# Router on one NeuronCore: attention answers stored in token order, with a 12-byte list entry per token and choice

## The chip, the cores and the metric

The kernel runs on one core of a Trainium2 chip. The metric is the device time of one execution in microseconds; the time shown for a kernel is the median of its runs. The core has five engines that each run their own instructions in order: TensorE (PE, with weight loads listed as PEld), VectorE (DVE), ScalarE (ACT), GpSimd (POOL) and SyncE (SP, which here only issues transfers). Transfers that need a list of row numbers (gathers and scatters) are issued by POOL, the plain ones by SP. All of them are moved by the same 16 DMA engines.

## The reference, cut to what matters

There are two parts. The first is a delta-rule attention over 768 steps for 4 batches of 8 heads of width 48; its answers, as 3072 tokens of 384 numbers, are the input of the second. The second is a mixture of 8 experts: each token is sent to the two experts with the largest noisy logits.

```python
# attention, for each batch and head
for t in range(S):
    y[:, :, t] = einsum('bhd,bhde->bhe', q[:, :, t], state)
    v_old = einsum('bhde,bhd->bhe', state, kt)
    state = state + bt * einsum('bhd,bhe->bhde', kt, vt - v_old)
# x: 3072 tokens of 384 numbers, D = 384, E = 8, F = 1024
logits = x @ w_gate
noisy_logits = logits + log1p(exp(x @ w_noise)) * noise
top2 = the two largest of noisy_logits;  top2_w = softmax over these two
for e in range(E):
    out[tokens of e] += top2_w * (relu(x[tokens of e] @ w1[e]) @ w2[e])
```

All numbers are 32-bit floats.

## The kernel before

**The attention stage** cuts the 768 steps into 12 chunks of 64. A unit is one chunk of two batches, 128 tokens, and there are 24 units; a step is four units, and there are 6 steps (0 to 5). Each step needs an inversion of small triangular matrices, which is done on DVE column by column (`invert`, with `column` at L705 to L717), and then a recurrence from unit to unit (`recur`, L838). `answer` (L943) makes the 128 token rows of a unit: ACT copies them into a tile of the ring `ys` (L482), and PE turns them and multiplies them by the router's weights.

**The router** (`route`, L1022) works for two steps at once, then two, then one and one (`ROUTES`). It chooses two experts for each token, and counts how many earlier tokens chose the same expert, which gives each token a slot in each of its two experts' lists.

**The lists.** `rows_x` is a DRAM tensor of 8 x 3072 rows of 388 numbers: the token's row of 384, its number, its two gates and a code for its first expert. SP first clears the beginning of each expert's list, 512 rows and then 320 more, with rows of zeros whose token number is N, which means none (`clear`, L378; placed behind columns of the first two inversions at L1359 to L1366). POOL then writes every token's row to its two slots (`spread`, L385), 48 scatters of 128 rows of 1552 bytes.

**The order of the attention stage** is made when the program is built. Every piece of work is a job with an engine, a cost and what it reads and writes (`Jobs.add`, L111). `Jobs.order` (L141) plays the jobs through with these costs and puts them in a fixed order on each engine: of the jobs that can start within 0.02 us of the earliest, it takes the one with the smallest key. A job with `late` has a key behind all jobs without, so it is taken only where nothing else can start on its engine. PSUM is handed out as two single banks and three pairs of banks.

**The early tiles.** Expert 0's list is worked on in tiles of 128 rows. Five of them are done with late jobs while the last tokens are still routed (`early`, L1227): `EARLY` (L26) says after which step which tiles are begun; after step 3 tiles 0 to 3 in two batches, after step 4 tile 4. `cut` (L1188) leaves empty slots so that those tiles are full at that point. A batch loads its rows with SP (`load_rows`, L1238), DVE reads number and gate from them (`of_rows`, L1254), PE turns them and multiplies by w1 (`inner_of`) and w2 (`back`), DVE multiplies by the gate (L1320), and POOL scatters the result into `out` (`put_early`, L1212).

**The experts.** `rest` (L1644) does the last 192 rows of expert 0, and then the loop over experts 1 to 7 follows; each has 832 rows in six tiles of 128 and one of 64. The products are done in the manner of Strassen and Winograd, with sums of blocks of the weights (`add_up`, on POOL for the experts from 2 on) and of the rows. SP loads the next expert's rows in two plain transfers (`load_rows`, L1537), `places` (L1550) reads numbers and gates from them, `turn_rows` (L1560) turns them on PE for the next expert, POOL gathers the sums so far from `out` (`gather`, L416) and scatters the new ones (`scatter`, L425). PE, ACT, DVE and POOL run in the written order here, and in the attention stage PE, ACT, DVE and SP do; POOL's jobs there are linked one behind the other.

Of the kernel before, what the change touches and what calls it, by code (L numbers as in the profile page):

```python
# [25 lines left out]
EARLY = {3: [(0, 2), (2, 4)], 4: [(4, 5)]}  # L26
EARLY_TILES = 5
ROWS = TILES * 128 + MORE
ROW = 384 + 4
# [65 lines left out]
class Jobs:  # L95
# [123 lines left out]

    PATIENCE = 0.02  # L220
    SOON = 8.0

    def run(self, link):

        last = None
        for job in self.order():
            made = job.emit()
            if job.engine == self.POOL:
                made = [x if isinstance(x, mybir.Instruction) else x.ins for x in made]
                if last:  # L230
                    link(last, made[0])
                last = made[-1]
# [3 lines left out]
def kernel(  # L236
# [87 lines left out]

    rows_x = tc.dram_tile([E * N, ROW], FP32, name="rows_x")
    empty = const.tile([128, ROW], FP32, name="empty")
    nc.vector.memset(empty, 0.0)
    nc.vector.memset(empty[:, DM : DM + 1], float(N))

    number = const.tile([128, NCH, NU], FP32, name="number")  # L330
    for i in range(2):
# [3 lines left out]
        )  # L335

# [39 lines left out]
    written, cleared, added, early_out = [], {"clear": [], "clear_more": []}, [], []  # L376

    def clear(e, lo, hi, p):  # L378

        return nc.sync.dma_start(  # L380
            out=rows_x[e * N + lo : e * N + hi].rearrange("(t p) d -> p t d", p=p),
            in_=empty[0:p, None, :].to_broadcast([p, (hi - lo) // p, ROW]),
        ).ins

    def spread(rows, slot, cleared, of):  # L385
        d = nc.gpsimd.indirect_dma_start(  # L386
            out=rows_x,
            out_offset=bass.IndirectOffsetOnAxis(ap=slot, axis=0),
            in_=rows,
            in_offset=None,  # L390
        ).ins
        tc.declare_no_dep(d, group="spread", reason="no two tokens have the same row")
        tc.add_to_no_dep_group("spread", d)
        for i in cleared:
            tc.add_manual_dep(d, i.name, SYNC, reason="rows cleared before they are written")
# [3 lines left out]

    def gates_of(xr, e, gate):  # L400

        nc.vector.scalar_tensor_tensor(
            out=gate, in0=xr[:, :, DM + 3], scalar=float(e - E), in1=xr[:, :, DM + 2],
            op0=ALU.is_equal, op1=ALU.mult,
        )
        nc.vector.tensor_tensor(out=gate, in0=gate, in1=xr[:, :, DM + 1], op=ALU.add)
# [26 lines left out]
    def deltanet(ictx):  # L433
# [47 lines left out]
        NY = 3  # L481
        ys = ring([128, US, ROW], "y", NY)  # L482
# [460 lines left out]
        def answer(n, bank_y):  # L943
# [4 lines left out]
            y_n = ys(s)[:, i, 0:DM]  # L948
            y_key, xT_key = ("y", s % NY, i), ("xT", n % 2)
# [36 lines left out]
            )  # L986
# [240 lines left out]
        def early(s, lo, hi):  # L1227
# [10 lines left out]
            def load_rows(at):  # L1238
# [3 lines left out]
                for of, w in written:  # L1242
                    if of <= s:
                        tc.add_manual_dep(d, w.name, SYNC, reason="rows of the tokens so far")
# [641 lines left out]
```

## Time and profile before

| | |
|---|---|
| median of 14 runs | 827.26 us (823.19 to 838.1) |
| the profiled execution's own time | 828.71 us |
| its span, first to last instruction | 827.0 us |
| mean granted TensorE clock | 0.885 |
| busy: PE, DVE, POOL, ACT | 740.8, 571.7, 360.4, 332.3 us |
| moved | 93.82 MB |
| attention and routing, until about | 317 us |
| early tiles of expert 0 on PE alone, until | 373 us |
| the last rows of expert 0, until | 394 us |
| experts 1 to 7 | 60.7 us each, until about 818 us |

Times inside the execution are counted from the first instruction. "L1532" is line 1532 of the kernel. A line of the timeline gives start, duration, engine, line, what is written from what, how many, and in brackets how long the engine was idle before and what ended that. A line of the stages gives for a stretch of time each engine's busy time with the number of its instructions, the granted clock of TensorE, the busy share of the 16 DMA engines, and GB/s.

### The profile page before, as it was taken

How to read it: one execution, taken by the hardware profiler on the slowest of the kernel's cores; microseconds unless marked ns; L12 is line 12 of the kernel's file. 1: busy time of each engine (PE TensorE's matmuls, PEld its weight loads, DVE VectorE, ACT ScalarE, POOL GpSimd, SP SyncE). 2: the span in 40 equal slices, each digit the busy share in tenths (PEclk: the TensorE clock that was granted, in tenths of full speed). 3: DMA queues.
4: the chain of work that ended last, by engine and by line, in shares of the span. 5: the costliest groups of instructions: out<-in, count | busy, mean ns of one | idle time of the engine just before them, and what ended most of it. 6: DMA issues, size and time to landing. Idle time of an engine off the chain costs nothing.

```text
span 827.0 us, 22812 instructions
## 1 busy us (share of the span) xinstructions
PE 740.8 (90%) x9510; PEld 586.7 (71%) x9510; DVE 571.7 (69%) x1295; ACT 332.3 (40%) x789; POOL 360.4 (44%) x372
## 2 busy tenths in 40 slices
PE   3565788986988889999999999999999999999995
PEld 2355687876877778767578588588588597597593
DVE  5899698899899754007695686675675776776751
ACT  3557185765765543112430530531530531521500
POOL 1102010106320634302773873873883774784411
PEclk8655567677689869999999999999999999999998
DMA  2469866455632413632723523424324323201201
GB/s 46 77 115 337 180 122 164 120 133 134 214 67 42 128 61 118 241 106 86 262 78 102 155 77 109 147 77 129 125 78 152 99 77 117 76 20 42 59 30 34
DMA packets 119856, 93.82 MB, mean 113 GB/s; under 512 B 85414, under 2 KB 110023, under 8 KB 119744
## 3 DMA queue, kind: packets, MB, share of 16 engines
q1 hardware_dynamic: 108016, 64.54, 28.5%
q0 software_dynamic: 9552, 27.33, 9.8%
q8 instruction: 77, 1.26, 0.6%
q10 hardware_dynamic: 2176, 0.39, 0.3%
q14 instruction: 35, 0.29, 0.1%
HBM read 58.82 MB, written 34.81 MB: 113 GB/s over the span
## 4 chain that ended last, share of the span: by engine, by line
PE 46%; issue 5%; POOL 2%; ACT 0%; POOLq 0%; ACTq 0%
PE inner L1532 25%; PE outer L1532 15%; PE inner L1637 2%; PE inner L1564 2%; POOL out_dram L427 1%; PE inner L1675 1%; POOL sums L418 1%; PE outer L1685 1%; POOL t_w L1505 0%; PE outer L1690 0%; PE outer L1675 0%; ACT xe_r L1668 0%; PE outer L1664 0%; ACT hT L1679 0%; POOLq L427 0%
## 5 line engine op out<-in xcount | busy, mean ns | idle before, releaser
L1591 DVE TENSOR_TENSOR hT<-hT,inner 128x416 f32<-128x416 f32 x182 | 105.4, 586 | 61.2 <-PE inner L1532 53.8
L1597 ACT ACTIVATE hT<-inner 128x416 f32<-128x416 f32 x112 | 57.9, 517 | 171.4 <-PE inner L1532 170.7
L427 POOL DMA_INDIRECT out_dram<-sums,index x49 | 50.8, 1037 | 113.7 <-DVE sums L1432 105.3
L1432 DVE SCALAR_TENSOR_TENSOR sums<-outer,gate,sums 128x192 f32<-128x192 f32 x112 | 45.2, 414 | 50.2 <-PE outer L1532 50.2
L1532 PE MATMUL inner<-s_x,w1e 128*128 128x416 f32 x196 | 78.8, 513 | 0.0
L710 DVE TENSOR_TENSOR part<-t 128x30 f32<-128x30 f32 (+9 forms) x180 | 67.7, 376 | 4.5
L714 DVE TENSOR_TENSOR t<-t,part 128x30 f32<-128x30 f32 (+9 forms) x180 | 65.4, 363 | 6.2
L1586 ACT ACTIVATE hT<-hT 128x416 f32<-128x416 f32 x112 | 59.9, 547 | 12.1 <-DVE hT L1591 6.9
L386 POOL DMA_INDIRECT rows_x<-y,slot x48 | 49.3, 1026 | 33.1 <-issue 8.8
L679 POOL TENSOR_SCALAR_AFFINE_SELECT t<-t 128x1024 f32<-128x1024 f32 x6 | 7.6, 1267 | 119.8 <-DVE ss L650 119.8
L1532 PE MATMUL outer<-t_w,hT 128*128 128x192 f32 x336 | 59.7, 328 | 0.0
L1532 PEld LDWEIGHTS inner<-s_x,w1e 128*128 128x128 f32 x196 | 37.2, 190 | 31.4 <-issue 29.6
L1532 PE MATMUL inner<-xe,w1e 128*128 128x416 f32 x140 | 58.1, 513 | 0.0
L418 POOL DMA_INDIRECT sums<-out_dram,index x49 | 51.8, 1057 | 13.8 <-issue 12.4
L1532 PE MATMUL inner<-s_x,s_w 128*128 128x416 f32 x140 | 56.9, 512 | 0.0
L1532 PEld LDWEIGHTS outer<-t_w,hT 128*128 128x128 f32 x336 | 54.7, 190 | 0.4
L1569 ACT COPY xe<-inner 128x384 f32<-128x384 f32 (+1 forms) x49 | 20.1, 462 | 85.4 <-PE inner L1564 85.2
L1532 PE MATMUL outer<-w2e,hT 128*128 128x192 f32 x280 | 50.1, 326 | 0.0
L861 POOL TENSOR_TENSOR v<-v,norms 128x384 f32<-128x384 f32 x24 | 21.9, 930 | 60.9 <-DVE norms L693 30.4
L1532 PEld LDWEIGHTS outer<-w2e,hT 128*128 128x128 f32 x280 | 46.5, 190 | 2.2 <-issue 2.2
L1498 POOL TENSOR_TENSOR w1e<-w1e 128x256 f32<-128x256 f32 x54 | 46.2, 865 | 2.0
L1532 PEld LDWEIGHTS inner<-s_x,s_w 128*128 128x128 f32 x140 | 26.6, 190 | 22.3 <-issue 22.3
(209 smaller groups left out, 1639.9 us busy)
## 6 DMA issues: line engine op xcount, KB each, us to landing
w1e<-in_moe_w_dram SPq DMA_DIRECT2D x8, 1536.0 KB
w2e<-in_moe_w_dram SPq DMA_DIRECT2D x8, 1536.0 KB
xr<-rows_x SPq DMA_DIRECT2D x7, 1164.0 KB
rows_x<-empty SPq DMA_DIRECT2D x8, 776.0 KB
qp<-in_q_dram SPq DMA_DIRECT2D x48, 96.0 KB
v<-in_v_dram SPq DMA_DIRECT2D x48, 96.0 KB
out_dram<-empty SPq DMA_DIRECT2D x4, 1152.0 KB
kp<-in_k_dram SPq DMA_DIRECT2D x88, 48.0 KB
```

The source lines that it names most:

```text
L386: d = nc.gpsimd.indirect_dma_start(out=rows_x, out_offset=bass.IndirectOffsetOnAxis(ap=slot, axis=0), in_=rows, in_offset=None,).ins
L418: nc.gpsimd.indirect_dma_start(out=got, out_offset=None, in_=out, in_offset=bass.IndirectOffsetOnAxis(ap=index, axis=0), bounds_check=N - ...
L427: nc.gpsimd.indirect_dma_start(out=out, out_offset=bass.IndirectOffsetOnAxis(ap=index, axis=0), in_=got, in_offset=None, bounds_check=N - ...
L710: v_.tensor_tensor(out=part, in0=t[:, :, j + 1 :, j, None].to_broadcast(shape), in1=t[:, :, None, j, 0:j].to_broadcast(shape), op=ALU.mult,)
L714: v_.tensor_tensor(out=t[:, :, j + 1 :, 0:j], in0=t[:, :, j + 1 :, 0:j], in1=part, op=ALU.add)
L861: lambda: [nc.gpsimd.tensor_tensor(out=v_n, in0=v_n, in1=norms(s)[:, i * H : (i + 1) * H, None].to_broadcast([128, H, D]), op=ALU.mult,)],
L1432: nc.vector.scalar_tensor_tensor(out=got, in0=p, scalar=gate, in1=got, op0=ALU.mult, op1=ALU.add)
L1498: engine.tensor_tensor(out=block(to), in0=block(x), in1=block(y), op=ALU.add if sign == "+" else ALU.subtract,)
L1532: nc.tensor.matmul(p, lhsT, rhs, start=opens and i == 0, stop=i == len(products) - 1, skip_group_check=True,)
L1586: nc.scalar.activation(h, h, ACTF.Relu)
L1591: nc.vector.tensor_tensor(out=h, in0=h, in1=p, op=ALU.add if sign > 0 else ALU.subtract)
L1597: nc.scalar.mul(h, p, float(sign))
```

## The change

The token rows are no longer carried in the lists. Each unit's answers are stored once, by SP, in a tensor `rows_y` of 3072 rows in the order in which they are made. A list entry (`tokens_x`) is now 12 bytes: token number, gate, and place in `rows_y`. One transfer fills all lists with empty entries. The experts load the entries (`load_metas`), DVE converts numbers and places to integers for all experts at once (`numbers`), and POOL gathers the rows by place, a tile at a time (`take_rows`). The code for the first expert and the arithmetic on it go, since an entry belongs to one choice and holds its own gate. `EARLY` begins tiles 0 and 1 after step 1. The zeroing of `out` moves from steps 2 and 4 to steps 1 and 2. The ring `ys` has four tiles of one unit each instead of three of four units. Two more tiles are zeroed by DVE at the start of the experts, since entries that are empty gather nothing. POOL's jobs in the attention stage are in the written order as those of the other engines.

```diff
-EARLY = {3: [(0, 2), (2, 4)], 4: [(4, 5)]}
+EARLY = {1: [(0, 2)], 3: [(2, 4)], 4: [(4, 5)]}
-ROW = 384 + 4
+META = 3
...
-    def clear(e, lo, hi, p):
-        return nc.sync.dma_start(
-            out=rows_x[e * N + lo : e * N + hi].rearrange("(t p) d -> p t d", p=p),
-            in_=empty[0:p, None, :].to_broadcast([p, (hi - lo) // p, ROW]),
+    def blank(tile):
+        blanked.append(
+            nc.sync.dma_start(
+                out=tokens_x.rearrange("(p t) c -> p t c", p=128), in_=tile
+            ).ins
+        )
+    def store(n, y_n):
+        d = nc.sync.dma_start(out=rows_y[n * 128 : (n + 1) * 128], in_=y_n).ins
+        tc.declare_no_dep(d, group="taken", reason="rows of other tokens were read")
+        stored.append((n, d))
+    def take_rows(got, index, units):
+        d = nc.gpsimd.indirect_dma_start(
+            out=got, out_offset=None, in_=rows_y[0 : units * 128],
+            in_offset=bass.IndirectOffsetOnAxis(ap=index, axis=0),
+            bounds_check=units * 128 - 1, oob_is_err=False,
         ).ins
+        tc.add_to_no_dep_group("taken", d)
+        for n, i in stored:
+            if n < units:
+                tc.add_manual_dep(d, i.name, SYNC, reason="rows stored before they are read")
+        return d
...
-        NY = 3
-        ys = ring([128, US, ROW], "y", NY)
+        NY = 4
+        ys = ring([128, DM], "y", NY)
...
+            jobs.add(
+                SP, 0.7, lambda: store(n, y_n), reads=[y_key], writes=[("stored", n)],
+                lands=2.0, moves=0.7,
+            )
...
-                        lambda x=x, of=of, i=i, to=to: [spread(
-                            ys(of)[:, i], to[:, x : x + 1],
-                            [y for name in clears for y in cleared[name]], of,
-                        )],
+                        lambda x=x, of=of, y=y, to=to: [
+                            spread(metas(g)[:, x, y], to[:, x : x + 1], of)
+                        ],
-                        due=FIRST + (s + paced) * PACE + BEHIND + 5.0, apart=4.5 / steps * paced,
+                        due=FIRST + (s + paced) * PACE + BEHIND + jobs.AFTER,
+                        apart=jobs.APART * paced,
...
+            jobs.add(
+                SP, 0.7, load_meta, reads=of_steps, writes=[("early_meta", lo)], lands=2.0,
+                moves=0.3, late=lo,
+            )
+            jobs.add(
+                DVE, 0.4, numbers, reads=[("early_meta", lo)], writes=[("early_index", lo)],
+                late=lo,
+            )
...
                 jobs.add(
-                    SP, 0.7, lambda at=at: load_rows(at), reads=of_steps,
+                    POOL, 1.2,
+                    lambda x=x, at=at: [take_rows(x, early_place[:, at : at + 1], units)],
+                    reads=[("early_index", lo), *(("stored", i) for i in range(units))],
                     writes=[x_key], lands=2.0, moves=0.7, late=lo,
                 )
...
-        for e in range(E):
-            for name, at, span in (
-                ("clear", (0, e * 4 + 1), (0, EARLIEST, 128)),
-                ("clear_more", (1, e * 3 + 2), (EARLIEST, ROWS, MORE)),
-            ):
...
+        behind(0, 20, 0.7, 1.0, lambda: blank(blanks), ["blank"])
-                (2, 4)[i // 2], (27, 29, 4, 16)[i], 0.7, 4.0, lambda i=i: clear_out(i),
+                (1, 2)[i // 2], (7, 22, 7, 22)[i], 0.7, 4.0, lambda i=i: clear_out(i),
...
-        for got in sums:
-            nc.gpsimd.memset(got, 0.0)
+        for got in (xrs[0], xrs[1], *sums):
+            (nc.vector if got in xrs else nc.gpsimd).memset(got, 0.0)
...
+        def numbers(e, t):
+            nc.vector.tensor_copy(places[:, e, t], metas[:, e, t, 2])
+            nc.vector.tensor_copy(indices[:, e, t], metas[:, e, t, 0])
+        def load_rows(e, tiles=range(TILES + 1)):
+            for i in tiles:
+                take_rows(
+                    xrs[e % 2][0 : rows_in[i], i], places[0 : rows_in[i], e, i : i + 1], NT
+                )
...
+            for e in range(E):
+                load_metas(e)
+            numbers(slice(0, 1), slice(t0, TILES + 1))
+            load_rows(0, range(t0, TILES + 1))
+            numbers(slice(1, E), slice(0, TILES + 1))
             load_rows(1)
             add_up(nc.vector, SUMS_W, blocks[0])
...
             if follows:
-                load_rows(e + 1)
                 weights = load_weights((w_even_tiles, w_odd)[(e + 1) % 2], e + 1)
                 blocks = blocks_of(*weights)
...
             first(a1, iter(of_hidden[0]))
             if follows:
+                load_rows(e + 1)
                 add_up(nc.gpsimd, SUMS_W, blocks[0])
```

The lists for tokens beyond the 832th of an expert (a branch at the end of the program) are changed in the same way; the branch is entered only where an expert has more rows than that. In this input the fullest expert has 807 tokens.

## The prediction

> **What bounds the kernel now.** I read the stages first, then who waits in each, then the timeline around every place the change touches. The columns are busy time with the number of instructions per engine, granted clock, DMA share and GB/s:
>
> ```profile
> 60.00:100.00 40.00, 26.08 (x800) 23.25 (x804) 32.09 (x74) 18.92 (x48) 4.99 (x5) 0.50 0.95 263
> 200.00:250.00 50.00, 42.95 (x1346) 37.60 (x1338) 45.49 (x108) 35.24 (x93) 19.18 (x20) 0.76 0.50 142
> 340.00:374.00 34.00, 32.27 (x150) 24.21 (x149) 2.72 (x8) 6.25 (x18) 2.96 (x3) 1.00 0.49 170
> 455.00:516.00 61.00, 61.00 (x288) 45.95 (x287) 42.17 (x76) 19.29 (x39) 41.08 (x40) 1.00 0.36 114
> ```
>
> Three regimes. Until about 280 us DVE sets the pace (third busy number: 45 of 50). From 316 us PE does, first with the early tiles of expert 0 (32 of 34), then with the experts, where it never rests. The chain that ended last agrees: back to 374 us it is nearly all PE. So time is won only by freeing DVE before 280 or by taking work from PE after 316.
>
> In the first stretch the DMA engines are full (0.95), and this shows in waits of PE and then DVE:
>
> ```profile
> PE pair L852 <- issue: 4.6, 1, 4.6
> PE pair L956 <- issue: 2.3, 1, 2.3
> DVE st L931 <- PE pair L919: 6.4, 2, 6.1
> ```
>
> PE's work after 316, from the timeline; the first batch (tiles 0 and 1) is the first two lines, most of it:
>
> ```profile
> 317.80 7.94 PE L1284 MATMUL pair<-early_xe,w1e 128*128 128x256 f32 x36
> 329.28 10.48 PE L1308 MATMUL pair<-w2e,early_hT 128*128 128x384 f32 x32
> 340.66 10.63 PE L1284 MATMUL pair<-early_xe,w1e 128*128 128x256 f32 x48 [0.57 <-ACT early_xe L1273]
> 368.02 5.33 PE L1308 MATMUL pair<-w2e,early_hT 128*128 128x384 f32 x16
> 373.38 0.62 DVE L1320 TENSOR_SCALAR early_x<-pair,early_gate 128x384 f32<-128x384 f32 x1 [11.05 <-PE pair L1308]
> 374.36 0.15 DVE L1470 CAST most_i<-most 128x1 int32<-128x1 f32 x1
> 375.23 4.67 POOL L1480 MEMSET sums<- 128x2688 f32 x2
> 375.51 5.14 PE L1675 MATMUL inner<-xe_r,w1e 128*128 128x192 f32 x30 [0.50 <-ACT xe_r L1668]
> ```
>
> The reader is to see that expert 0's last rows start at 375.51, 2.16 us after PE's last early matmul (368.02 + 5.33 = 373.35, called T), as their rows were loaded long before.
>
> **Lists: clears go, stores come.** Out go 8 x (776 + 485) KB = 10.1 MB that SP issues from 60 to 107 us. In come 0.3 MB of empty entries, 24 stores of 192 KB from 81 us on, and the 4.6 MB that zero `out`, drawn forward from 133 to 217. I put about 5.5 MB in the old clears' stretch, so the queues are no longer full, and I expect DVE's 6.1 us wait at 94 to 100 to shrink to about 1: **-5 us** (ends: 0, as "issue" names no cause, and -9.2, the waits 2.3 + 2.3 + 4.6 of PE at 77 to 90). A store takes SP about 0.67 us (four v loads took 2.67) and waits for ACT's copy; behind it on SP stand q, k and v loads, and POOL's v products and then DVE wait for those. SP often waits on PE for their buffers anyway: **0**, ends 0 and +5 (the nearest row: POOL's v product waited 3.99 us for its v before 113.81). The zeroing of `out` is four issues of 0.66, moved ahead of loads of steps 2 and 3 on SP; only the early scatters wait for it, which come after 225: 0. The router loses one DVE subtraction of 0.17 per route and POOL four small copies: 0. The 48 scatters stay 48 at 0.97 us; only their pieces shrink.
>
> **Tiles 0 and 1 begin after step 1.** Their 7.94 + 2.84 + 10.48 = 21.3 us of PE leave the stretch after 316: **-21.3**. They go beside the recurrences at 225 to 316, where PE is idle about 7 of 50 us, at a clock of 0.76. Their weights are there (issued at 146.7 and 163.8), the 16 scatters of steps 0 and 1 ran from 192.7 to 215 with one at 233. With them go 8 ACT relus of 0.38, two DVE products of 0.62, two casts of 0.15, four POOL transfers of 1.0. What it costs there is not shown. Ends: -2 (steadier matmuls lift the clock: 1.00 in all of 316 to 374) and +21.3 (nothing hidden). Three in-order queues are crossed: on SP the entry load waits for the last of the 16 scatters to land, with v and q loads of step 4 behind it (before, such loads held SP 50.8 us in all with nothing behind them); on POOL the gathers and two scatters stand among v products; on DVE the casts among columns. I take **+3.5**, nearest the lower end: 21.3 us of jobs of about 1.3 us, each of which can hold back a recurrence step, with DVE's columns as cover while they last (to 277).
>
> **Tiles 2 and 3 take one hop more.** Now SP loads rows and PE turns them. Then: entries, two casts, a gather of 1.0 us, 3.1 us to land. The entries land as the rows did (313.1); casts 0.3, signal 0.3, gather and landing 3.1, the second 1.3 later, against a fourth row load that landed at 315.5: **+3** (ends 0, and +9 where seven scatters of 1.27 are put first on POOL). POOL's scatters of step 4, which wait here for the reads of the list (7.46 us idle until 316.31), still do. Tile 4 waited for the buffer of tile 0; it no longer does: 0.
>
> **Expert 0's last rows now wait for DVE and POOL after T.** `numbers` and `take_rows` stand behind the early jobs on in-order engines. DVE: product and counts to T+1.2, then two zeroings of 128x2688, by POOL's row of that shape 2.35 each, to T+5.9, casts to T+6.3. POOL: scatter, then its own two zeroings (375.23 + 4.67) to T+6.6; gathers issue at T+6.6 and T+7.9, land 3.1 later at T+11.0; transpose 0.5, copy 0.3, signals 0.4: matmuls start at T+12.2, not T+2.2: **+10** (ends +8, landing 2.5 and faster zeroing, and +14, landing 6.7, the slowest of that row). PE's clock falls in such a gap: after the last matmul (817) it is 0.54 on average in 821 to 827; and it climbs from 0.50 through 0.81 to 1.00 in 304 to 316, one 4-us slice: **+2**, ends 0 and +4. Expert 1's seven gathers follow to T+18.3 and land by T+21.4; PE wants them from T+12.2+8.1 on, tile by tile: 0. The eight entry loads are about 6500 pieces of 12 bytes. The 16 k loads of the first 10 us are 4096 pieces of 192 bytes at a DMA share of 0.46, at most 18 ns each on one engine: 7.3 us over 16 engines, between the last scatter's landing (341) and T: 0.
>
> **Experts 2 to 7: seven gathers more on POOL.**
>
> ```profile
> 412.20 0.95 POOL L418 DMA_INDIRECT sums<-out_dram,index  x1 [0.30 <-DVE s_h L1520]
> 413.18 1.41 POOL L1498 TENSOR_TENSOR w1e<-w1e 128x256 f32<-128x256 f32 x2
> 420.58 1.54 POOL L1498 TENSOR_TENSOR s_w<-w1e,s_w 128x256 f32<-128x256 f32 x2 [4.58 <-PE inner L1532]
> 437.95 1.00 POOL L427 DMA_INDIRECT out_dram<-sums,index  x1 [0.30 <-issue]
> 444.19 1.41 POOL L427 DMA_INDIRECT out_dram<-sums,index  x1 [5.24 <-DVE sums L1432]
> L418 POOL DMA_INDIRECT sums<-out_dram,index x49: 953/999/1417, 404.3 to 775.6; - x49
> ```
>
> 7 x 1.30 = 9.1 us stand before the weight sums. POOL waits 4.58 and 5.24 = 9.8 us there, so the third scatter still goes at about 444, and the sums end at 441 where the next expert starts at 455. The rows land by 426, PE turns the first at 430. Cost 0 (ends 0 and +2.2 an expert, if all gathers took 1.42: 7 x 0.42 less the 0.7 that is left).
> The Trainium skill speaks against this ("DMA: Bandwidth & Descriptors", SWDGE vs HWDGE vs iDMA): POOL writes the descriptors of its transfers to SBUF, and DVE can lock it out there in its two-port mode. Where the lock held each gather to the slowest shown, the sum would be 13 us worse; the row's median of 999 ns, beside a DVE busy 42 of 61, says it hardly does, and I go by the row.
> The same page (Rules for kernel authors) advises against many small transfers; it prices no 12-byte piece, so the 18 ns above stands.
>
> **Sum.** -5 - 21.3 + 3.5 + 3 + 10 + 2 = -7.8: the profiled 828.71 (span 827.0 and 1.7 around it) becomes 820.9. That execution lies 1.45 above the median, so I predict 819.5.
>
> **Rivals.**
> *Late jobs starve.* A late job runs only where its engine has nothing else. DVE is idle under 0.7 us in most 10-us slices from 225 to 280, so the casts of tiles 0 and 1 may come only after 277. The batch then fills PE's gaps at 280 to 316: in clock-weighted work PE does 22.4 of 36 us there, so 13.6 of 21.3 fit and 7.7 remain instead of 3.5: -3.6, or 824. For: DVE's fullness; against: the boundary of an inversion at 229 to 236, where DVE waits on ACT.
> *A pair of banks is held (the slower side).* The product that empties a tile's bank pair is a late DVE job too. If it waits for 277 while PE is done early, one or two of three pairs are lost to the recurrences of step 4, which need two at a time. Step 4's recurrence (236 to 282) would slip; at half of these 46 us the sum is -7.8 + 23 = +15: 842. It decides from 12 us of slip, where the sum passes +4. Against: the order is made with these costs.
> *The lists were hidden anyway and the hops are longer.* No gain from the clears, +9 and +14 at the upper ends: -21.3 + 3.5 + 9 + 14 + 2 = +7: 834.
> *More from the queues.* With -9.2, insertion at -2 and no hop: -21.3 - 9.2 - 2 + 10 + 2 = -20: 807.
>
> **How the numbers follow.** Forecast 0.40, own range 813 to 825; starved 0.22; pair held 0.18; hidden 0.12; more 0.08. Two runs of this kernel differ by about 0.5%, 4.1 us, and less can't be told from none. Faster: 0.9 of the forecast, 0.4 of starved, all of more: 0.53; slower: pair held, 0.9 of hidden, little of the rest: 0.30; same 0.17. The range leaves out the farthest of pair held and of more: 808 to 839.
>
> **What would show it.** No "issue" wait over 2 us at 77 to 95, and a DMA share under 0.8 there; L1284 before 280; matmuls of tile 2 within 4 us of the attention's last; PE idle about 10 us before L1675's successor with two DVE zeroings in it; experts at 60.7 us. Wrong, if attention ends more than 8 us from 317, or that gap is not 8 to 14.

## The result, and the profile after

The changed kernel takes 848.43 us (median; 843.29 to 858.02), the kernel before 829.36 (823.19 to 839.46): a ratio of 1.0238 (95% interval 1.0205 to 1.0270), 19 us slower. I had predicted 819.5 with a range of 808 to 839.

The profiled execution took 848.97 us, its span is 847.2, 20.2 more than before. Where they lie, from the timelines of both:

| place | before | after | adds |
|---|---|---|---|
| end of PE's last early matmul, T | 373.35 | 374.97 | +1.6 |
| from there to the first matmul of expert 0's last rows | 2.2 | 12.6 | +10.5 |
| those 30 matmuls | 5.14 | 7.78 | +2.6 |
| from the start of expert 1 to the last scatter | 423.2 | 423.6 | +0.4 |
| from the start of the last scatter to the end of the span | 9.6 | 14.7 | +5.1 |

The last column adds up to 20.2; between the third row and the fourth lie 13.6 us in both kernels. Of the five rows, two were in the prediction with about the right size (+10 and +2), the experts stood there with 0, T with -19.8, and the last row was not in it at all. The last scatter, first before, where the span is 827.0 us, then after:

```profile
817.44 0.98 POOL L427 DMA_INDIRECT out_dram<-sums,index  x1 [0.32 <-DVE sums L1432]
```
```profile
832.54 0.97 POOL L442 DMA_INDIRECT out_dram<-sums,indices  x1 [0.33 <-DVE sums L1439]
```

The view by stretches of the changed kernel (columns as before: busy time with instructions of PE, PEld, DVE, ACT, POOL, the granted clock, DMA share, GB/s):

```profile
60.00:100.00 40.00, 27.39 (x980) 24.41 (x983) 38.18 (x82) 22.42 (x58) 7.68 (x8) 0.67 0.57 146
...
200.00:250.00 50.00, 45.35 (x1204) 39.84 (x1206) 42.06 (x100) 31.30 (x86) 10.54 (x12) 0.64 0.22 47
340.00:375.00 35.00, 33.76 (x159) 25.18 (x157) 1.85 (x3) 6.63 (x19) 10.12 (x11) 1.00 0.38 109
375.00:388.00 13.00, 1.85 (x8) 1.28 (x8) 11.67 (x26) 0.79 (x2) 9.84 (x7) 0.67 0.20 47
470.00:531.00 61.00, 61.00 (x287) 45.69 (x286) 39.21 (x70) 19.29 (x39) 47.97 (x47) 1.00 0.35 112
```

The reader is to see this. With the clears gone the DMA share at 60 to 100 is 0.57 instead of 0.95, and DVE is busy for 38.2 us instead of 32.1. PE's stretch after the attention is as full as it was. And there is a new stretch, 375 to 388, in which PE does 1.85 us in 13 while DVE and POOL are busy. In an expert POOL works 48.0 of 61 us instead of 41.1, and PE rests as little as before.

Then the timeline of tiles 0 and 1 and of the time behind T (start, busy time, engine, line; in brackets the idle time before it and what ended it):

```profile
224.56 0.38 SPq L1257 DMA_DIRECT2D early_meta<-tokens_x  x1
279.40 0.12 DVE L1266 CAST early_place<-early_meta 128x2 int32<-128x2 f32 x1
288.06 1.05 POOL L396 DMA_INDIRECT early_x<-rows_y,early_place  x1 [0.31 <-issue]
290.74 1.05 POOL L396 DMA_INDIRECT early_x<-rows_y,early_place  x1 [0.30 <-issue]
320.25 9.31 PE L1310 MATMUL pair<-early_xe,w1e 128*128 128x256 f32 x42
330.43 10.57 PE L1334 MATMUL pair<-w2e,early_hT 128*128 128x384 f32 x32
342.28 10.63 PE L1310 MATMUL pair<-early_xe,w1e 128*128 128x256 f32 x48 [0.62 <-ACT early_xe L1299]
369.64 5.33 PE L1334 MATMUL pair<-w2e,early_hT 128*128 128x384 f32 x16
376.58 2.30 DVE L1491 MEMSET xr<- 128x2688 f32 x1 [0.51 <-DMA metas<-tokens_x]
376.86 4.65 POOL L1491 MEMSET sums<- 128x2688 f32 x2
379.39 2.30 DVE L1491 MEMSET xr<- 128x2688 f32 x1 [0.51 <-issue]
381.60 0.10 DVE L1561 CAST places<-metas 128x2 int32<-128x2 f32 x1
382.58 1.05 POOL L396 DMA_INDIRECT xr<-rows_y,places  x1 [1.08 <-issue]
385.82 1.39 PE L1672 MATMUL outer<-ident,xr 128*128 128x128 f32 x6 [10.74 <-DMA xr<-rows_y,places]
387.62 7.78 PE L1683 MATMUL inner<-xe_r,w1e 128*128 128x192 f32 x30 [0.41 <-ACT xe_r L1676]
```

The entries of tiles 0 and 1 are loaded at 224.6, 86 us earlier than their rows were before (310.6), as the change means it. Then they wait: DVE's casts come at 279.4, the gathers at 288 and 291, and PE's matmuls at 318 to 341, right where they were. The later lines are the stall: two zeroings on DVE, the casts, the gather, and PE idle for 10.74 us until the rows are there.

### The profile page after: what moved, and what is told of

Same layout as the page of the kernel before. It is cut to its first block, busy times and chain, and to the rows that moved or that the text cites. A ratio compares the mean times of both kernels' runs of the same rounds, so it can differ in the third digit from the quotient of the medians.

```text
span 847.2 us, 22977 instructions
## 1 busy us (share of the span) xinstructions
PE 748.6 (88%) x9512; PEld 591.2 (70%) x9512; DVE 556.6 (66%) x1240; ACT 332.1 (39%) x789; POOL 416.8 (49%) x432
## 3 DMA queue, kind: packets, MB, share of 16 engines
q0 software_dynamic: 11472, 27.31, 10.9%
## 4 chain that ended last, share of the span: by engine, by line
PE 63%; DVE 16%; issue 9%; ACT 3%; POOL 3%; DMA 2%; SPq 2%; POOLq 0%; DVEq 0%; ACTq 0%
PE inner L1543 24%; PE outer L1543 15%; DVE part L725 5%; DVE t L729 4%; PE pair L1310 3%; PE pair L1334 3%; PE pair L594 3%; PE inner L1647 2%; PE inner L1574 2%; DMA kp<-in_k_dram 1%; SPq L528 1%; PE single L986 1%; PE inner L1683 1%; DVE t L644 1%; PE pair L971 1%
## 5 line engine op out<-in xcount | busy, mean ns | idle before, releaser
L442 POOL DMA_INDIRECT out_dram<-sums,indices x51 | 54.7, 1072 | 99.0 <-DVE sums L1439 78.0
L1439 DVE SCALAR_TENSOR_TENSOR sums<-outer,metas,sums 128x192 f32<-128x192 f32 (+1 forms) x113 | 46.0, 416 | 63.8 <-PE outer L1543 62.9
L408 POOL DMA_INDIRECT tokens_x<-meta,slot x48 | 47.6, 991 | 76.7 <-DVE r_d L1058 40.2
L396 POOL DMA_INDIRECT xr<-rows_y,places x51 | 56.1, 1099 | 16.3 <-issue 15.4
L433 POOL DMA_INDIRECT sums<-out_dram,indices x49 | 51.2, 1046 | 13.9 <-issue 13.5
```

Of the source, the lines that this page charges most:

```text
L396: d = nc.gpsimd.indirect_dma_start(out=got, out_offset=None, in_=rows_y[0 : units * 128], in_offset=bass.IndirectOffsetOnAxis(ap=index, ax ...
L408: d = nc.gpsimd.indirect_dma_start(out=tokens_x, out_offset=bass.IndirectOffsetOnAxis(ap=slot, axis=0), in_=meta, in_offset=None, bounds_c ...
L433: nc.gpsimd.indirect_dma_start(out=got, out_offset=None, in_=out, in_offset=bass.IndirectOffsetOnAxis(ap=index, axis=0), bounds_check=N - ...
L442: nc.gpsimd.indirect_dma_start(out=out, out_offset=bass.IndirectOffsetOnAxis(ap=index, axis=0), in_=got, in_offset=None, bounds_check=N - ...
L1439: nc.vector.scalar_tensor_tensor(out=got, in0=p, scalar=gate, in1=got, op0=ALU.mult, op1=ALU.add)
```

## The experiments

Each one changes the kernel after unless it says otherwise. Two kernels with the same order in the attention can end it several us apart in their profiles (more on that below), so I read the effect in the stage first and the total second.

### The wait behind the last early matmul

Zero only what the first gathers need, and the rest behind them:

```diff
-        for got in (xrs[0], xrs[1], *sums):
-            (nc.vector if got in xrs else nc.gpsimd).memset(got, 0.0)
+        nc.vector.memset(xrs[0][:, EARLY_TILES:], 0.0)
...
             load_rows(0, range(t0, TILES + 1))
+            nc.vector.memset(xrs[1], 0.0)
             numbers(slice(1, E), slice(0, TILES + 1))
             load_rows(1)
+            for got in sums:
+                nc.gpsimd.memset(got, 0.0)
+            nc.vector.memset(xrs[0][:, 0:EARLY_TILES], 0.0)
```

> Theory (the stall after the early matmuls is real and sets the end): with only the two last tiles of the row buffer zeroed ahead of the gathers, and the other zeroings behind them, DVE reaches the casts about 2.0 us after the last early matmul instead of 6, the gathers go at 2.4 and 3.7, land by 6.8, and expert 0's last matmuls start 8 us after it instead of 12.6: 4 to 5 us less than the changed kernel, 843.5 to 844.5. Rival (expert 1's gathers, which then stand before POOL's zeroings of the sums, or something else behind the stall is late anyway): within 1.5 us of 848.4.

Measured: T at 379.30, the matmuls at 387.17, a gap of 7.9 us instead of 12.6, as the theory said. From T to the last scatter it takes 452.2 us instead of 457.6. The total did not show it: 848.99 us, ratio 1.0245 (1.0158 to 1.0333). In the profiled run the attention had ended 4.3 us later, 324.7 instead of 320.4, though the edit leaves the attention's order as it was. From its timeline:

```profile
380.51 0.70 DVE L1490 MEMSET xr<- 128x768 f32 x1
385.38 1.38 PE L1675 MATMUL outer<-ident,xr 128*128 128x128 f32 x6 [5.97 <-DMA xr<-rows_y,places]
```

So next the whole hop goes ahead of T: entries, casts and gathers of these rows become jobs behind the last list scatter, into two tiles of their own. The zeroings of `sums` and of the first row buffer go behind the gathers, and PE multiplies by w2 ahead of turning expert 1's rows.

```diff
+            jobs.add(SP, 1.4, load_meta, reads=[("rows", x, i, y) ...], late=4.15, ...)
+            jobs.add(DVE, 0.4, numbers, reads=["rest_meta"], late=4.15, ...)
+            for i, size in enumerate((128, MORE)):
+                jobs.add(POOL, 1.2, lambda ...: [take_rows(rest_x[i][0:size], ...)], late=4.15)
...
-        for got in (xrs[0], xrs[1], *sums): ...
+        nc.vector.memset(xrs[1], 0.0)
...
-            for i in range(TILES + 1):
-                turn_rows(1, i, range(5))
-            add_up(nc.vector, SUMS_X, xb)
...
+            for i in range(TILES + 1):
+                turn_rows(1, i, range(5))
+            add_up(nc.vector, SUMS_X, xb)
```

> The entries, casts and gathers of expert 0's last 192 rows become jobs ahead of the end of the early tiles, into buffers of their own, and expert 0's product with the second weights runs ahead of expert 1's transposes. Theory (the wait after the early matmuls, 10.5 us more than before and 2.6 us of slow matmuls behind it, is worth 13 us of the end): these matmuls start within 3 us of the last early one, and the kernel takes 833 to 839. Rival (expert 1's rows, gathered only then, become the new wait): the gap closes but expert 1 starts only 4 to 8 us earlier, 840 to 845.

Measured: 840.18 us, ratio 1.0184 (1.0100 to 1.0268). The gap is 2.2 us (373.3 to 375.46) and expert 1 starts 22.5 us after T instead of 34.0, but it takes 65.5 us instead of 60.8: PE waits 2.5 us there for sums that DVE makes of rows that were gathered late, and has a clock of 0.66 in the 5 us behind that. The rival was right about the total, the theory about the gap. So four of expert 1's seven tiles are gathered ahead too, the zeroing of the other row buffer goes to POOL, and PE's order is that of the changed kernel again:

```diff
+            for i in range(4):
+                jobs.add(POOL, 1.2, lambda ...: [take_rows(xr_1[0:128, i], ...)], late=5.0, ...)
...
+            load_rows(1, range(4, TILES + 1))
+            for x in (*sums, xrs[0]):
+                nc.gpsimd.memset(x, 0.0)
```

> As the run with the hoisted gathers, with the first four tiles of expert 1 gathered ahead of the end of the early tiles too, the zeroing of the other row buffer moved to POOL, and the order of PE's work as in the changed kernel. Theory (what was left of the stall had moved into expert 1, 65.5 us instead of 60.8): the first matmuls of the last rows start within 3 us of the last early one, expert 1 starts 20 to 22 us after it and takes 60.9 us; the kernel takes 833 to 837, 13 us less than the changed kernel. Rival (POOL's six gathers in front of the early scatters push these out and hold up the tiles' buffers): 838 to 842.

Measured: 838.77 us, ratio 1.0128 (1.0076 to 1.0181). The gap is 2.1 us, the matmuls run at full clock again, expert 1 starts 20.8 us after T and takes 60.8:

```profile
378.66 0.88 PE L1740 MATMUL outer<-ident,rest_x 128*128 128x128 f32 x6 [0.66 <-DVE counts L1548]
380.00 5.14 PE L1751 MATMUL inner<-xe_r,w1e 128*128 128x192 f32 x30 [0.46 <-ACT xe_r L1744]
```

From T to the last scatter it takes 444.2 us, as the kernel before does (444.1), where the changed kernel takes 457.6: the stall is worth 13.4 us of the end. The total fell by 9.7 only, and in the profile the attention ended at 323.3.

### Tiles 0 and 1

Put only the batches back where they were:

```diff
-EARLY = {1: [(0, 2)], 3: [(2, 4)], 4: [(4, 5)]}
+EARLY = {3: [(0, 2), (2, 4)], 4: [(4, 5)]}
```

> Only the early batches are put back to steps 3 and 4, as before the change; storage, gathers and everything else stay changed. Theory (late jobs starved: tiles 0 and 1 ran behind the attention all the same): the time stays at 848.4 within 2.5 us, and the attention's last matmuls stay near 318.9. Rival (the entry load, the casts and the gathers that were drawn forward took the attention's 11 us away again): attention ends 6 to 11 us earlier, 837 to 842.

Measured: 851.87 us, ratio 1.0282 (1.0200 to 1.0363), the attention's last matmul at 322.4. Taking the move back makes no difference that these runs can tell: the move did nothing. Why it did nothing is in the planner's order: these jobs have the key of late jobs, behind every other job that can start. So give tiles 0 and 1 a due time:

```diff
+            def urgent(late):
+                return {"due": FIRST + (s + 2) * PACE + BEHIND} if s == 1 else {"late": late}
...
-                SP, 0.7, load_meta, ..., late=lo,
+                SP, 0.7, load_meta, ..., **urgent(lo),
...
```

> The jobs of tiles 0 and 1 get a due time in the middle of step 4's recurrences instead of the key that puts them behind all others. Theory (only the order starved them): their first matmuls run before 290 us, at least 10 of their 21.3 us of PE leave the stretch after the attention, and the kernel takes 832 to 840. Rival (a pair of banks and PE's time are really needed by the recurrences): the attention's end moves out by as much as the tail gets shorter, or by more: 846 to 865.

Measured: 854.46 us (854.07 without the slowest of its four runs), ratio 1.0299 (1.0210 to 1.0388). The batch ran at 242 to 276, but the attention ended at 338.4, 18 us later, and T came at 380.0. From its timeline, and the waits of DVE from 230 to 300 (line waited for: us, times, longest):

```profile
242.55 5.70 PE L1313 MATMUL pair<-early_xe,w1e 128*128 128x256 f32 x24
248.09 5.32 PE L1337 MATMUL pair<-w2e,early_hT 128*128 128x384 f32 x16
```
```profile
DVE st L946 <- PE pair L934: 12.4, 2, 11.3
DVE v L896 <- PE pair L594: 3.3, 2, 2.1
```

PE's 21 us in front of step 4's recurrences held those back by nearly their whole length; DVE waits 11.3 us in one piece for the product that updates the state. One step later:

```diff
-                return {"due": FIRST + (s + 2) * PACE + BEHIND} ...
+                return {"due": FIRST + (s + 3) * PACE + BEHIND} ...
```

> As the run in which tiles 0 and 1 were not late, but due one step later (44 us in the planner's time). Theory (PE and its banks have no room beside the recurrences, wherever the batch is put): the stretch after the attention is 19 to 21 us shorter and the attention ends 15 to 21 us later than 320, so 846 to 856. Rival (only the place was wrong, in front of step 4's recurrences): the attention ends under 10 us later, 836 to 842.

Measured: 843.37 us, ratio 1.0165 (1.0103 to 1.0228), T at 369.2, 5.7 us earlier than in the changed kernel. The attention ended 19 us later (339.5), as the theory said, yet the stretch behind it shrank by more, 29.7 us instead of 54.6, as part of tiles 2 and 3 already ran before that end. The total lies between the two expectations: of the 17.8 us that I had counted, about 5 were to be had, with the later of the two due times that I tried. The interval touches that of the changed kernel (1.0205 to 1.0270), so the 5 us are not firm.

Does the move pay without the rest of the change? The kernel before, with the batch of tiles 0 and 1 after step 1 and the same due time:

```diff
-EARLY = {3: [(0, 2), (2, 4)], 4: [(4, 5)]}
+EARLY = {1: [(0, 2)], 3: [(2, 4)], 4: [(4, 5)]}
```

> The kernel before with nothing but its early batches: tiles 0 and 1 after step 1 instead of 3, with the due time of e10. Theory (the move as such is worth what e10 gained over the changed kernel, 5 to 6 us, and costs nothing at the end, as rows are loaded by SP and POOL has no transfer more): 822 to 825 where the kernel before takes 829, the gap between the last early matmul and expert 0's last rows stays at 2.2 us and the end at 9.6 us. Rival (e10 gained because PE's stretch after the attention was longer there, or its profile was a lucky one): 827 to 831.

Measured, on a chip on which the kernel before took 855.55 us: 869.44, ratio 1.0163 (1.0116 to 1.0209). Neither theory nor rival: it costs 14 us. The longest waits of DVE from 186 to 316 in its profile:

```profile
DVE missing L1194 <- PE single L1204: 13.8, 1, 13.8
DVE v L881 <- PE pair L579: 12.2, 4, 10.9
```

The 13.8 us end at 307.1 and belong to the second cut of the list, the one after step 3, which needs a count from PE; at the cut after step 1 DVE waits 4.1 us, until 198.2. In the changed kernel neither cut waits (185.2 and 275.0). There is no profile of the kernel before on this slower chip, so how much of these waits is the move's stays open. The move gained 5 us in one order and cost 14 in another: a run of one order says little of another.

### Clears and stores

Put the old 10 MB of zeros back, at their old places in SP's order, to a DRAM tensor that nobody reads:

```diff
+        for e in range(E):
+            for name, at, span in (
+                ("clear", (0, e * 4 + 1), (0, EARLIEST, 128)),
+                ("clear_more", (1, e * 3 + 2), (EARLIEST, ROWS, MORE)),
+            ):
+                behind(*at, 0.7, (span[1] - span[0]) * 0.0052, lambda ...: clear(e, *span), ...)
```

> The changed kernel with the old 10 MB of zeros written as before, at the same places in SP's order, to a DRAM tensor that nobody reads. Theory (the clears held up DVE until 126 us, but the attention's end is set by what PE and DVE do later): the inversion that starts at 126 comes at 134 to 138 again, yet the attention ends within 4 us of 320 to 325, and the kernel takes 846 to 852. Rival (the gain is carried to the end and something else in the change ate it): the attention ends 9 to 11 us later, 857 to 860.

Measured: 851.88 us, ratio 1.0331 (1.0251 to 1.0410), the inversion that starts at 126 in the changed kernel at 148.7, later than either the kernel before (137.3) or my 134 to 138, the attention's end at 325.6. Up to 137 us the kernel before spends 77.3 us from 60 on, with DVE busy 65.6 of them; the changed one reaches the same inversion after 66.4 us with 62.7: 11.8 us of idle DVE became 3.8. What became of these 8 us is in the stretch from 186 to 216, the end of a step. First the kernel before, then the changed kernel, its busy times, DVE's waits from 186 to 241 and the longest of them in the timeline, then the changed kernel with the clears put back:

```profile
60.00:137.33 77.33, 59.22 (x1838) 53.06 (x1840) 65.57 (x153) 45.85 (x119) 8.98 (x10) 0.61 0.78 197
...
186.00:216.00 30.00, 23.39 (x779) 20.99 (x779) 27.54 (x63) 16.97 (x43) 19.98 (x22) 0.68 0.63 182
```
```profile
60.00:126.45 66.45, 48.05 (x1763) 42.56 (x1763) 62.68 (x147) 44.59 (x116) 8.89 (x10) 0.73 0.57 152
186.00:216.00 30.00, 22.16 (x653) 19.24 (x649) 19.93 (x46) 17.12 (x44) 16.55 (x17) 0.65 0.36 62
```
```profile
DVE st L946 <- ACT kT L583: 5.5, 1, 5.5
DVE v L896 <- PE pair L594: 3.4, 2, 1.9
```
```profile
212.53 0.38 PE L594 MATMUL pair<-kT 64*64 64x64 f32 x4 [2.27 <-issue]
...
214.82 1.11 PE L934 MATMUL pair<-u,kp 64*64 64x48 f32 x32
...
216.06 0.56 DVE L946 TENSOR_TENSOR st<-pair,st 128x384 f32<-128x384 f32 x1 [5.47 <-ACT kT L583]
```
```profile
60.00:100.00 40.00, 24.23 (x736) 21.47 (x736) 32.80 (x73) 18.14 (x47) 4.99 (x5) 0.54 1.01 288
...
186.00:216.00 30.00, 25.86 (x722) 22.89 (x726) 28.32 (x72) 16.57 (x40) 17.45 (x18) 0.70 0.41 79
```

With the clears DVE works 28.3 of these 30 us, without them 19.9: it comes early and then waits for the recurrences, which PE does at a clock of 0.65. The profile puts the 5.5 us down to ACT's copy of k, the last to report; the product that this update adds to the state, PE's L934, ends just before it too. It stands in PE's order behind products of other units and a pause of 2.27 us for which the profile names no cause, and which of these held it isn't shown. The kernel before has 27.5 there (25.9 with the 49 idle gathers of the last experiment on the end of the program); every profile of the changed kernel's attention without the clears, whatever else differed, has 19.9 to 23.3. DVE's state updates tell the same: the second of a pair starts at 198.80 before and at 187.95 after, a lead of 10.9; the next ones are 2.8, 1.9 and, at the end, 3.1 us ahead (223.01 to 220.24, 246.10 to 244.22, 305.74 to 302.66). Beside the run with the clears, which differs in nothing else, the leads are 11.3, 5.4, 3.8, 2.1, 2.7 and, at the end, 2.0 us (199.29, 225.63, 248.04, 264.95, 282.46 and 304.63 there). The clears' removal moved the stall, and little of it reached the end of the attention. Whether the 5 us by which the run with the clears ended later are theirs I can't say, since its clock was at 0.50 from 300 to 320, which alone moves that end (below).

Three things that the change put in the attention, one at a time. The stores on ACT's queue:

```diff
-        d = nc.sync.dma_start(out=rows_y[n * 128 : (n + 1) * 128], in_=y_n).ins
+        d = nc.scalar.dma_start(out=rows_y[n * 128 : (n + 1) * 128], in_=y_n).ins
...
-                SP, 0.7, lambda: store(n, y_n), ...
+                ACT, 0.1, lambda: store(n, y_n), ...
```

> The 24 stores of the answers go from SP's queue to ACT's, right behind the copy they need, so that q, k and v loads no longer stand behind a store that waits. Theory (the stores on SP gave the 11 us back that the clears' removal had won by 126 us): inversion 5 ends 4 to 9 us earlier than 275.2 and the kernel takes 838 to 844. Rival (DVE and PE lost them to the order of the products and of POOL): 847 to 850; if the issues cost ACT 0.6 us each where it is full, up to 855.

Measured: 847.26 us, ratio 1.0251 (1.0172 to 1.0331); the attention's end at 317.5. No stores at all:

```diff
-            jobs.add(SP, 0.7, lambda: store(n, y_n), reads=[y_key], writes=[("stored", n)], ...)
...
-            out=got, out_offset=None, in_=rows_y[0 : units * 128],
+            out=got, out_offset=None, in_=rows_v[0 : units * 128],
```

> The 24 stores of the answers are left out, and the gathers read rows of a weight tensor in their place, so the numbers that the experts compute are not the reference's; lists, counts and all other transfers stay. Theory (the stores cost the attention what the clears had cost): the inversions of 171 and 226 come 3 to 5 us earlier, the attention ends at 312 to 316, and the kernel takes 842 to 845. Rival (the loss is in the order of DVE's and PE's work at the end of a step): within 2.5 us of 848.4.

Measured: 849.40 us (845.83 without the slowest of its four runs), ratio 1.0249 (1.0180 to 1.0319). Eight buffers for the answers:

```diff
-        NY = 4
+        NY = 8
```

> Eight buffers for the answers instead of four (the kernel before had room for twelve). Theory (an answer can't be copied before the store of the fourth one before it has left, so stores and copies hold each other up): the attention ends 3 to 6 us earlier, 842 to 845. Rival: 848.4 within 2.5 us; ACT's copies of the answers waited for PE alone in the trace.

Measured: 844.24 us, ratio 1.0194 (1.0153 to 1.0235), the attention's end at 319.2. The old distance between the list scatters:

```diff
-                        apart=jobs.APART * paced,
+                        apart=4.5 / steps * paced,
```

> The list scatters at the old distance in the planner's time, 4.5 us over the steps of a route, instead of 2.0. Theory (denser scatters stand between POOL's products of v and hold DVE up at 280 to 300): the idle time of DVE there, 6.3 and 6.4 us, shrinks by half and the attention ends 3 to 6 us earlier, 842 to 846. Rival: 848.4 within 2.5 us, or slower, as the last scatters of a route come later and tiles 2 and 3 wait for them.

Measured: 847.11 us, ratio 1.0239 (1.0199 to 1.0279). The stores and the distance are worth nothing that can be measured. The buffers may be worth the 4 us that they showed; the intervals overlap, and the attention ended only 1.2 us earlier in the profile, so this stays open. None of the three is a second cause of the stall at 186 to 216.

### The end of the program

The 5.1 us after the last scatter hold no instruction of the kernel in the profile. One suspect is the block for experts with more than 832 tokens, which is skipped there. Both kernels without it:

```diff
-    with tc.If(count > ROWS):
-        for e in range(E):
-            ...
```

> The kernel before without the block for experts with more than 832 tokens, which this input never enters (the output needs it only for other inputs). Theory (leaving the program past that block costs the time after the last scatter): the 9.6 us from the last scatter to the end fall to 5 to 8, and the kernel is 2 to 5 us faster than before. Rival (that time is the landing of the last scatters and the end of the program): 9.6 stays within 1 us. Beside that it shows how far the attention's end (317.6) moves from run to run: if by 4 us or more, differences of that size between the two kernels there are no effect of the change.

> The changed kernel without the same block. Theory (the block): its 14.7 to 15.2 us after the last scatter fall to the same 5 to 8 as in the kernel before without it, 7 to 9 us less than 848. Rival (what POOL's transfers leave behind): 14.7 stays, and the time stays within 2 us of 848.

Measured: before without the block 821.91 us, ratio 0.9971 (0.9933 to 1.0010), after without it 841.17, ratio 1.0221 (1.0128 to 1.0314). The last scatter and the span of each, first before, then after:

```profile
core 0: 818.4 us, clock 0.903
```
```profile
813.08 0.98 POOL L427 DMA_INDIRECT out_dram<-sums,index  x1 [0.32 <-DVE sums L1432]
```
```profile
core 0: 836.6 us, clock 0.904
```
```profile
826.44 0.97 POOL L442 DMA_INDIRECT out_dram<-sums,indices  x1 [0.33 <-DVE sums L1439]
```

9.6 us become 5.3, and 14.7 become 10.2: the block costs 4.3 and 4.5 us at the end of either kernel, and the difference of 5 stays. The attention of the kernel before, which this edit leaves alone, ended at 313.2 here, 4.4 us earlier than in the first profile (317.6). The second suspect is the number of POOL's indirect transfers, 153 before and 209 after. The kernel before with 49 more, of rows nobody uses:

```diff
+            for i, p in enumerate(rows_in):
+                nc.gpsimd.indirect_dma_start(
+                    out=spare[0:p, i], out_offset=None, in_=w2_rows[0:N],
+                    in_offset=bass.IndirectOffsetOnAxis(ap=index[0:p, i : i + 1], axis=0),
+                    bounds_check=N - 1, oob_is_err=False,
+                )
```

> The kernel before with 49 gathers more on POOL, 7 in each of experts 1 to 7, of rows that nobody uses, right where the changed kernel gathers. Theory (the time from the last scatter to the end grows with the number of POOL's indirect transfers, 153 before and 209 after the change): it goes from 9.6 to 13.5 to 14.7 us and the kernel takes 4 to 5 us more than before, all of it there; the experts stay at 60.7. Rival (something else of the change, the 12-byte pieces or the bounds check, makes the end longer): 9.6 within 1 us, and the time as before.

Measured: 833.41 us against 831.50 of the kernel before beside it, ratio 1.0046 (1.0008 to 1.0084), with the experts at 60.7 to 61.0.

```profile
core 0: 828.5 us, clock 0.917
```
```profile
813.64 0.98 POOL L427 DMA_INDIRECT out_dram<-sums,index  x1 [0.32 <-DVE sums L1432]
```

From the last scatter to the end it is 14.9 us instead of 9.6. This is the cause of the 5.1: the changed kernel has 56 transfers more, and 49 more cost 5.3 us here, some 0.1 us each, all of it after the last one is done. What that time is spent on, no view shows. The total rose by less, 1.9 us by the medians, where I had expected 4 to 5; its interval holds up to 7.

### The repairs together

> The hoisted gathers of e11 and the later due time for tiles 0 and 1 of e10 together. Theory (the stall and the place of tiles 0 and 1 are independent): 848.4 - 9.7 - 5 = 833 to 835, still 3 to 6 us above the kernel before, which is the 5 us at the end of the program. Rival (the new late jobs on POOL and DVE and the batch among the recurrences compete): 837 to 842.

The hoisted gathers and the later due time in one kernel: 831.38 us, ratio 1.0038 (1.0000 to 1.0077). By the totals they add up, 17 us below the changed kernel, and what is left above the kernel before is less than the 15.1 us at the end explain (5.5 more than 9.6). In the profile they do not quite: T comes at 368.8, but the hoisted gathers are issued only at 367.2 and 368.5, PE waits 2.7 us for their rows, the gap is 4.3 us and the 30 matmuls take 7.7 again, so that 5.3 of the 13.4 us are back. It does not beat the kernel before.

## Why the prediction was wrong, point by point

**Tiles 0 and 1 begin after step 1: -21.3 + 3.5.** This is the step that failed, 17.8 of the 28 us between the sum (-7.8) and what was measured (+20.2). I checked that the data would be there (it was, at 224.6) and that PE had idle time, and did not ask where the planner's order puts a job with the key of a late one. On PE it put the batch behind the last recurrence. My rival had the starving and the late casts (279.4, after its 277), but took the casts for its cause and let 13.6 of the 21.3 us run between 280 and 316; none did. The insertion cost was wrong as well, +3.5 where PE seemed idle 7 of 50 us. Pushed forward, the batch cost the attention 18 and 19 us, nearly the upper end of 21.3. PE's idle time there was no free room.

**Clears go: -5.** The place and the size were right where I looked: the DMA share fell to 0.57, and DVE's wait of 6.4 us for PE's state products is gone. What failed is the step from there to the end. I had read DVE as the bound until 280; from 186 to 216 the next in line is the recurrence, and DVE is idle there for the 8 us that it had won. Of a lead of 11.3 us over the run with the clears 2.0 were left at the last state update, and the attention ended no earlier than before.

**Stores: 0.** Right: no stores at all made no difference that can be measured (ratio 1.0249 beside 1.0238).

**One hop more for tiles 2 and 3: +3.** From the attention's last matmul to T it takes 54.6 us, 55.8 before: 0. The hop is hidden, since tiles 0 and 1 still stood in front of it: the rows are gathered at 319 and 322, and PE turns them at 341.

**Expert 0's last rows: +10, and +2 for the clock.** Right, 10.5 and 2.6, and by the steps given: the casts at T+6.6 (T+6.3 predicted), the first gather at T+7.6 (6.6), the rows 3.1 us later, the matmuls at T+12.6 (12.2). With the hop hoisted it all went.

**Expert 1's gathers and the entry loads: 0.** Right as it stood; in the hoisted kernel, where PE came earlier, they did become late (65.5 us).

**Seven gathers more in every expert: 0.** Right: experts at 60.7 to 60.9 us. POOL's sums end 46.9 us into the expert (441 - 394.2 = 46.8 predicted), the third scatter goes 50.2 us into it, 50.0 before.
The lock that the Trainium skill warns of ("DMA: Bandwidth & Descriptors", SWDGE vs HWDGE vs iDMA) cost the experts nothing: the 51 gathers have a median of 998 ns, beside a DVE that is busy 39 of 61 us, and the longest took 1.70 us. What made some longer, no run shows.

**What was not in the sum: the end, +5.1.** I counted what the gathers cost beside the experts and took their end for granted, with 9.6 us from last scatter to end in the trace of before and no row to say what is in it. This term was put at nothing without a reason; the runs showed 0.1 us for each transfer.

With what was measured, T as one term, the sum is 1.6 + 10.5 + 2.6 + 0.4 + 5.1 = +20.2. The slower side that I had at 842 was another mechanism than the one that came.

## What to carry to other kernels

An order that is written out ahead decides when a moved job runs: find its place on each engine's queue (above all on the engine that does most of its work) before the time it leaves behind is counted as won. A wait that goes is worth what the next bound lets through, so follow the lead into the next stretch where another engine sets the pace. And a hop through three in-order queues behind a common event costs its whole length there; hoist it, as here for 13 us.

## What the runs showed of the hardware

Each of POOL's indirect transfers added about 0.1 us after the last one (49 more: 9.6 to 14.9 us), and a block of code that is never entered added 4.3 to 4.5 us there.

The attention's end moves with the granted clock as much as with the edits. Two profiles of the same order, first the one with the zeroings rearranged, then the one without the skipped block:

```profile
300.00:310.00 10.00, 9.44 (x207) 8.28 (x206) 4.14 (x13) 1.31 (x4) 0.00 (x0) 0.50 0.07 23
310.00:320.00 10.00, 10.00 (x156) 9.29 (x156) 2.14 (x14) 3.07 (x8) 2.58 (x3) 0.50 0.13 26
```
```profile
300.00:310.00 10.00, 9.15 (x304) 8.29 (x300) 4.95 (x18) 2.66 (x8) 0.00 (x0) 0.96 0.08 26
310.00:320.00 10.00, 9.88 (x116) 8.87 (x116) 4.58 (x27) 4.75 (x15) 5.09 (x5) 1.00 0.36 67
```

PE is as busy in both, at 0.50 in the one and 0.96 to 1.00 in the other, and the attention ends at 324.7 and at 316.0. The Trainium skill ("TensorE: Matmul & The Clock Gate", Part 1) has two states of the clock, half and full, set by PE's activity in windows that run on their own; these rows agree with the two levels. That activity sets them the rows don't show, since PE is busy for more than 9 of 10 us at either level; what holds the clock at half here stays open. A difference of under 9 us in one profile of this stage therefore can't be put down to an edit, which is why the 5 us of the run with the clears stay open. The same holds for the +1.6 of T in the first table: the kernel before ended its attention at 317.6, 313.2 and 312.0 in the three profiles that leave it as it was (the last is the one with the idle gathers), the changed kernel at 320.4, 324.7 and 316.0, so the change may cost some us there that I can't assign.
